# Reordering one block's VectorE queue: a sum ahead of the gain multiply, scalings behind the sums, a gain multiply one group later

## The chip, the cores and the metric

The kernel runs on one core of a Trainium2 chip. The metric is the device time of one execution in microseconds (us). Before the change it is 321.7 us, the median of 4 runs (321.48 to 322.55).

## What is computed

A linear attention without softmax is followed by a gated feed-forward layer. The batch is 8, with 8 heads, 576 tokens and a head width of 64; the layer takes the 4608 tokens as rows of 512.

```python
kv = einsum('bhsd,bhse->bhde', k, v)
o = einsum('bhsd,bhde->bhse', q, kv)
x = o / sqrt(mean(o * o, axis=-1) + 1e-06) * g_norm      # rows of 512 = 8 heads x 64
g, val = x @ w_gate, x @ w_val                            # 512 -> 1536
ffn = gelu(g) * val @ w_out                               # 1536 -> 512
out = x + sigmoid(x @ w_res) * ffn
```

## The kernel before, in words

**Blocks and batches.** The work is cut into nine blocks of 512 tokens: block b (0 to 7) is the first 512 tokens of batch b, and block 8 holds the 64 remaining tokens of every batch. While the feed-forward work of block m fills TensorE (PE), the attention of a later batch is threaded into it. Batch 2 is prepared in block 1, and batches 3 to 7 are prepared two blocks ahead, so batch 3 is begun in block 1 and finished in block 2.

**Order of the work.** There is no automatic scheduler. The program runs under a manual schedule: every engine does its instructions in the order in which they are written, and waits only where an operand or a buffer isn't ready. The order is put together from dictionaries. `at(block, slot, ...)` puts a step into a slot of a block. `aside_out(block, word, ...)` and the dictionary `amid_out` put one ahead of a named point of the output stage (`others`, in `out_by_products`). `at_word(block, i, word, ...)` puts one behind a named word of the i-th group of the gate and value stage (`gv_group`).

**The gate and value stage.** In block 2 and later it is done in three groups (i = 0, 1, 2) of 4 x 128 hidden columns. Each group computes gate (g) and value (v) by a scheme of seven half-size products instead of eight. Its order is a string of words. A digit is a product on PE (L946, 4 matmuls of 128x256). `E` is a copy of A into the bank of E on ScalarE (ACT, L956). `d` is a copy of F into SBUF on ACT (L960). `F` and `c` are sums A + d on VectorE (DVE, L967). `g11` and its like are gelus on ACT (L977). `h11`, `h12`, `h21` are products into `hid` on DVE, and `h22` is one on GpSimd (POOL), all L983. In block 2, group 0 has the order None, group 1 False, group 2 True:

```python
None:  "1g 1v Eg 5g 6g Ev 5v dg 6v dv Fg 2g Fv 2v 7g g11 7v cg 3g cv 3v h11 g12 4g g21 h12 4v g22 h21 h22"
False: "1g 1v Eg 5g Ev 5v dg 6g dv 6v Fg 2g Fv 2v 7g g11 7v cg 3g cv 3v h11 g12 4g g21 h12 4v g22 h21 h22"
True:  "1g 1v Eg 5g Ev 5v dg 6g dv 6v Fg 2g Fv 2v 7g g11 7v cg 3g cv 3v h11 g22 4g g12 h12 4v g21 h22 h21"
```

Products 1, 6, 7 and 4 all accumulate into the bank of A. So product 6 waits until the copy `E` has read A, product 7 until the sum `F` has read it, product 4 until the sum `c` has. Product 5 and then the sum `F` write the bank of F; product 2 adds to E and product 3 to F.

**Banks.** PSUM has eight banks, and all are in turn. The attention result of batch 3 (tiles `op`, o[0] to o[3]) lies in four of them at the end of block 1. In group 0 of block 2 the F tiles of g and v take the banks of o[0] and o[1]; in group 1 the A tiles of g and v take those of o[2] and o[3] (`banks_of`). From one group to the next E and F change places: the E tile of v in group 2 takes the bank of the F tile of v in group 1, and so the copy `Ev` of group 2 (L956) waits until `h12` of group 1 (L983 on DVE) has read that.

**The output stage of block 1** (`others`) does five more products of 12 matmuls (L515): wA, wE, wA, wF, wA. Its first lines, with the points at which other steps come in, are:

```python
prod(w["A"], s_[1], wo_t[:, 1], False)
aside("F")
sub(nc.vector, w["F"], w["A"], w["d"], ALU.add)
...
aside("00")
prod(w["E"], a_of(blk, 1, 2), b_of(2, 1), False)
```

The next product into wA waits until the sum into wF (L478 on DVE) has read wA. At "00" and at "end" two `token_sums` each of block 2 stand (tile `ts`, L478). The gated outputs `osb<-th,w...` (L698) stand between.

**The attention steps that matter here.** `a_norm` computes the inverse norms `ny` from the sums of squares `ss` by twelve small operations on POOL (L306 to L319). `a_t(b, i)` scales o[i] by `ny` into the tile `t` (L345, DVE) and so frees the bank of o[i]. `d_xT` sends `t` through a transposing DMA from the queue of SP into `xT` (L387). `a_g(b, j0, j1)` multiplies `xT` by the gain vector in place (L370, a DVE tensor_scalar of 128x1024 in fp16). Meanwhile POOL does `row_times_g` (L361, four operations on `t`) and in group 1 `fin` (L702, four additions on `osb`), both of 128x512.

Of the kernel before, what the change touches and what calls it, by code (L numbers as in the profile page):

```python
# [18 lines left out]
def kernel(  # L19
# [19 lines left out]
    F = moe_w_gate.shape[1]  # L39
    NP = H // 2  # L40
    NF = F // P
    NJ = 4
# [85 lines left out]
    def by_token(b, copy=nc.vector.tensor_copy, js=slice(0, NJ)):  # L128
        copy(
            out=b16_t[b, "q"].rearrange("p j h d -> p h j d")[:, :, js, :],  # L130
            in_=raw[b, "q"].rearrange("p h (j d) -> p h j d", j=NJ)[:, :, js, :],
        )
# [36 lines left out]
    def attn_begin(b):  # L169
        st[b] = {  # L170
            "qT": attnp.tile([P, NJ, NP, P], FP16, tag="qT", bufs=1, name="qT"),
            "kv2": (
                attnp.tile([P, NP, D], FP16, tag="kv2", bufs=4, name="kv2")
                if b > 0
                else t_t[B][:, NJ - 1, :].rearrange("p (r c) -> p r c", r=NP)
            ),
            "ss": attnp.tile([P, NJ + 1, H], FP32, tag="ss", name="ss"),
            "o": {},
        }
# [36 lines left out]
    def a_kv(b, copy=nc.vector.tensor_copy):  # L216
        ps = pattn.tile([P, NP, D], FP32, tag="at", name="kvp")
        kv_mm(b, ps)
        copy(out=st[b]["kv2"], in_=ps)
# [18 lines left out]
    def of_o(ap, i):  # L238

        jj, e = i // 2, i % 2  # L240
        return ap[:, 2 * jj : 2 * jj + 2].rearrange("p j (r e) -> p j r e", e=2)[:, :, :, e]
# [85 lines left out]
    def pair(b):  # L327

        return b - B // 2 if b >= B // 2 else None

    def where(b, j):
        return (b, j) if j < NJ else (B, pair(b))

    def a_t(b, i):

        o, rinv = st[b]["o"][i], st[b]["rinv"]
        if i < NJ:
            jj, e = i // 2, i % 2
            t = t_t[b][:, 2 * jj : 2 * jj + 2, :].rearrange("p j (r e d) -> p j r e d", e=2, d=D)[:, :, :, e, :]
            scale = of_o(rinv, i)[:, :, :, None].to_broadcast([P, 2, NP, D])  # L340
        else:
            t = t_t[B][:, pair(b), :].rearrange("p (h d) -> p h d", h=H)
            o = o.rearrange("p (h d) -> p h d", h=H)
            scale = rinv[:, NJ, :, None].to_broadcast([P, H, D])
        nc.vector.tensor_tensor(out=t, in0=o, in1=scale, op=ALU.mult)  # L345
# [17 lines left out]
    def a_g(b, j0, j1, eng=nc.vector):  # L363

        blk, k0 = where(b, j0)
        xs = xT_t[blk][:, k0 : k0 + j1 - j0, :, :]
        if eng is nc.scalar:
            nc.scalar.activation(out=xs, in_=xs, func=AF.Copy, scale=gcol)
        else:
            eng.tensor_scalar(out=xs, in0=xs, scalar1=gcol, scalar2=None, op0=ALU.mult)  # L370


    def d_qT(b):
        nc.sync.dma_start(
            out=st[b]["qT"].rearrange("p j c t -> p (j c) t"),
            in_=b16_t[b, "q"].rearrange("p j h d -> p (j h d)"),
            transpose=True,
        )
# [5 lines left out]
    def d_xT(b, j0, j1):  # L384
        blk, k0 = where(b, j0)
        k1 = k0 + j1 - j0
        nc.sync.dma_start(  # L387
            out=xT_t[blk][:, k0:k1, :, :].rearrange("p j c t -> p (j c) t"),
            in_=t_t[blk][:, k0:k1, :].rearrange("p j c -> p (j c)"),
            transpose=True,  # L390
        )
# [638 lines left out]
    for which in "kv":  # L1030
        if which == "k":
            t = hidp.tile([P, NF, NJ * P], FP16, tag="hid", name=which + "f").rearrange("p a b -> p (a b)")
        else:
            t = hid_s
# [8 lines left out]
    for which in "kv":  # L1043
        t = hid_of[which]
# [295 lines left out]
    amid_out = {}  # L1340
# [3 lines left out]
    def load_behind(b, x_of=None):  # L1344

        nc.gpsimd.tensor_copy(out=hold, in_=st[b]["qT"][0:1, 0, 0, 0:1])
        if x_of is not None:
            nc.gpsimd.tensor_copy(out=hold, in_=xT_t[x_of][0:1, 0, 0, 0:1])
        if pair(b) is not None:
            nc.gpsimd.tensor_copy(out=hold, in_=st[b]["qrT"][0:1, 0, 0:1])  # L1350
        load_batch(b + 1)

    def at(blk, slot, *fs):
        plans[blk].setdefault(slot, []).extend(fs)

    def aside_out(blk, ahead_of, *fs):
        amid_out.setdefault(blk, {}).setdefault(ahead_of, []).extend(fs)

    def plan_attn_2():
        b, m = 2, 1  # L1360
        act = nc.scalar.copy
        at(m - 1, 2 * NF + 3, lambda: by_token(b, act, slice(0, 2)))
        at(m, 0, lambda: by_token(b, act, slice(2, 4)), lambda: attn_begin(b), lambda: d_qT(b))
        at(m, 2, lambda: a_kv(b))
        at(m, 3, lambda: load_behind(b))
        at(m, 1, lambda: wo_sums(1))
        at(m, 3, lambda: wo_sums(3))
        at(m, 4, lambda: a_o(b))
        for j in range(NJ):
            at(m, 4 + j // 2, lambda j=j: a_ss(b, j))  # L1370
        at(m, 6, lambda: a_norm(b, 0, NJ, nc.gpsimd))
        for j in range(NJ):
            at(m, 9 + j // 2, lambda j=j: a_t(b, j))
        at(m, 10, lambda: d_xT(b, 0, NJ))
        for i in range(2):
            aside_out(m, "F", lambda i=i: a_g(b, 2 * i, 2 * i + 2))

    WHOLE = 2
    GROUPS = {blk: (1, 2) for blk in range(2, WHOLE)} | {blk: (0, 1, 2) for blk in range(WHOLE, B - 1)} | {B - 1: (1, 0, 2), B: (0, 1, 2)}
# [2 lines left out]
    def at_word(blk, i, word, *fs):  # L1382
        amid_gv.setdefault((blk, i), {}).setdefault(word, []).extend(fs)
# [5 lines left out]
    def plan_attn_ahead(b):  # L1389

        rem = pair(b) is not None
        m = b - 2
        assert rem == (m in GROUPS)
        act, pool = nc.scalar.copy, nc.gpsimd
        begin = [lambda: attn_begin(b), lambda: d_qT(b)]
        if rem:
            at_word(m, 0, "h22", begin.pop(0), lambda: d_rem_qT(b))
        if m in GROUPS:
            for i in range(2):
                half = lambda i=i: by_token(b, act, slice(2 * i, 2 * i + 2))  # L1400
                if whole(m):
                    at_word(m, i, "g11", half)
                else:
                    at(m, 2 + i, half)
            if whole(m):
                at_word(m, 1, "g11", *begin)
            else:
                at(m, 3, *begin)
            if b + 1 < B:
                at(m, 2 * GF, lambda: load_behind(b))  # L1410
            last = len(GROUPS[m]) - 1
        else:
            at(m, 8, lambda: by_token(b, act, slice(0, 2)))
            at(m, 9, lambda: by_token(b, act, slice(2, 4)), *begin)
            at(m, NF - 1, lambda: a_kv(b, act))
            at(m, NF, lambda: load_behind(b))
        if rem:
            at_word(m + 2, 0, "cv", lambda: a_g(b, NJ, NJ + 1))
            own = 2 * pair(b) + 1 == b
            at_word(m, last, "5v" if own else "3g", lambda: a_rem_kv(b))  # L1420
            at_word(m, last, "dv" if own else "g12", lambda: kv_out(b))
            if own:
                at_word(m, last, "3g", lambda: rem_mm(b))
            at_word(m, last, "g12", lambda: rem_out(b))
        else:
            at(m, NF, lambda: a_o(b), lambda: a_ss(b, 0), lambda: a_ss(b, 1))
            aside_out(m, "D", lambda: a_ss(b, 2), lambda: a_ss(b, 3))
        aside_out(m, "F", lambda: a_norm(b, 0, NJ + rem, pool))
        first = [lambda: new_block(b), lambda: a_t(b, 0), lambda: a_t(b, 1)]
        if whole(m + 1):  # L1430
            aside_out(m, "01" if m + 1 == WHOLE else "11", *first[0:2])
            amid_out[m].setdefault("end", []).insert(0, first[2])
        else:
            at(m, NF + 3, *first)
        if whole(m + 1):
            t = [lambda j=j: a_t(b, j) for j in range(NJ)]
            if rem:
                at_word(m + 1, 0, "h21", lambda: a_t(b, NJ), lambda: d_xT(b, NJ, NJ + 1))
            for i, word, fs in (
                (0, "1v", t[2:3]),  # L1440
                (0, "Fv", [t[3], lambda: d_xT(b, 0, NJ)]),
                (1, "cv", [lambda: a_g(b, 0, 2)]),
                (2, "Fv", [lambda: a_g(b, 2, NJ)]),
            ):
                at_word(m + 1, i, word, *fs)
            return
        for j in range(2, NJ + rem):
            at(m + 1, j - 2, lambda j=j: a_t(b, j))
        at(m + 1, 1, lambda: d_xT(b, 0, NJ))
        at_word(m + 1, 1, "Fv", lambda: a_g(b, 0, 2))  # L1450
        at_word(m + 1, 1, "cv", lambda: a_g(b, 2, NJ))
# [12 lines left out]
    for blk in GROUPS:  # L1464
        t = token_sums(blk, nc.vector)
# [170 lines left out]
```

## Time and profile before

| what | value |
|---|---|
| median of 4 runs | 321.7 us (321.48 to 322.55) |
| time of the profiled execution | 330.97 us |
| its span, first to last instruction | 329.2 us |
| PE, DVE, ACT, POOL busy in the span | 314.6 (96%), 279.8 (85%), 210.9 (64%), 186.4 (57%) us |
| mean granted PE clock | 0.989 |
| 4 matmuls of 128x256 back to back (chain) | 0.44 us |
| 12 of them (chain) | 1.31 us |
| block 1's last products and block 2, and where block 3 begins | 82.31 to 124.89 us |

The profile is of one execution. Its span runs from the first instruction to the last; 1.77 us of its time lie outside. A row of the timeline gives the start, the time from start to end, the engine, the line in the code, the operation, the tile written and the tiles read; in brackets stands how long the engine had been idle and what ended that. The chain of waits is followed back from the last instruction: each piece is what the next one had to wait for, or what preceded it on the same engine. Where a piece of four matmuls takes longer than 0.44 us, PE waited in it.

### The profile page before, as it was taken

The page shows a single profiled execution, that of the slowest core. Times are in us where ns is not written, and L with a number is a line of the kernel's source. Part 1 is how long each engine was busy: PE and PEld are TensorE (multiplying, and loading weights), DVE is VectorE, ACT ScalarE, POOL GpSimd, SP SyncE. Part 2 cuts the span into 40 slices and gives each one's busy share as a digit, 9 for nine tenths or more (in the row PEclk, how much of TensorE's full clock was granted, in tenths as well). Part 3 has the DMA queues.
Part 4 walks back from the last instruction along what each step waited for, and adds up shares of the span by engine and source line. Part 5 has one row for each costly group of instructions (what it writes and reads, how often), then busy time and mean ns, then how long its engine had stood idle before and what let it go on. Part 6 is the DMA issues. An engine that isn't in the chain of part 4 may idle for free.

```text
span 329.2 us, 7756 instructions
## 1 busy us (share of the span) xinstructions
PE 314.6 (96%) x3044; PEld 248.2 (75%) x3044; DVE 279.8 (85%) x486; ACT 210.9 (64%) x385; POOL 186.4 (57%) x249
## 2 busy tenths in 40 slices
PE   8899999999999999999999999999999999399993
PEld 3545755445888888888888888888888888268882
DVE  6788889798897999899989997999896778947774
ACT  3773676465568776877687678766764668026770
POOL 3792342573778568866786678147812753805432
PEclk9999999999999999999999999999999999959999
DMA  7999999899977594669366937202400030000304
GB/s 247 323 190 204 194 205 174 179 201 135 197 77 94 163 191 53 124 162 188 53 132 155 182 37 164 96 2 55 155 2 0 3 128 2 0 2 7 122 0 129
DMA packets 76694, 38.90 MB, mean 118 GB/s; under 512 B 42098, under 2 KB 74354, under 8 KB 76658
## 3 DMA queue, kind: packets, MB, share of 16 engines
q0 software_dynamic: 38752, 17.17, 41.4%
q1 hardware_dynamic: 37328, 20.71, 24.8%
q8 instruction: 24, 0.39, 0.5%
q10 hardware_dynamic: 578, 0.52, 0.5%
q14 instruction: 12, 0.10, 0.1%
HBM read 38.80 MB, written 9.44 MB: 147 GB/s over the span
## 4 chain that ended last, share of the span: by engine, by line
PE 90%; DVE 5%; DMA 2%; SPq 1%; issue 1%; POOL 0%; ACT 0%; DVEq 0%
PE Av L946 12%; PE Ag L946 12%; PE wA L515 11%; PE Fv L946 6%; PE Fg L946 6%; PE gps L410 5%; PE vps L410 5%; PE rA L566 4%; PE fps L447 3%; PE Ev L946 3%; PE Eg L946 3%; PE wE L515 3%; PE wD L515 3%; PE w L515 2%; PE wF L515 2%; DVE ts L478 2%
## 5 line engine op out<-in xcount | busy, mean ns | idle before, releaser
L983 POOL TENSOR_TENSOR hid<-ge,c 128x512 f16<-128x512 f16 x22 | 25.6, 1162 | 49.6 <-ACT ge L977 49.6
L515 PEld LDWEIGHTS <-hid_s 128*128 128x128 f16 x384 | 37.5, 98 | 4.5 <-issue 0.2
L946 PEld LDWEIGHTS <-wsv 128*128 128x128 f16 x352 | 34.2, 98 | 5.8 <-issue 1.3
L946 PEld LDWEIGHTS <-wsg 128*128 128x128 f16 x352 | 34.7, 99 | 4.4
L515 PEld LDWEIGHTS <-hid 128*128 128x128 f16 x288 | 28.7, 100 | 10.2 <-issue 6.2
L361 POOL TENSOR_TENSOR t<-t,g 128x512 f16<-128x512 f16 x32 | 35.9, 1151 | 0.0
L956 ACT COPY Eg<-Ag 128x512 f32<-128x512 f32 x22 | 12.8, 583 | 35.7 <-PE Ag L946 35.7
L702 POOL TENSOR_TENSOR osb<-osb,t 128x512 f32<-128x512 f32 x28 | 34.1, 1248 | 0.0
L946 PEld LDWEIGHTS <-wg 128*128 128x128 f16 x264 | 26.0, 99 | 3.4
L967 DVE TENSOR_TENSOR Fg<-Ag,d 128x512 f32<-128x512 f32 x22 | 15.3, 697 | 15.5 <-ACT d L960 7.6
L946 PEld LDWEIGHTS <-wv 128*128 128x128 f16 x264 | 26.0, 99 | 3.2
L946 PE MATMUL Av<-ts,wsv 128*128 128x256 f16 x176 | 26.4, 272 | 0.2 <-ACT Ev L956 0.2
L946 PE MATMUL Ag<-ts,wsg 128*128 128x256 f16 x176 | 26.4, 273 | 0.0
L258 DVE TENSOR_REDUCE ss<-sq 128x8 f32<-128x512 f32 x32 | 20.5, 679 | 1.7 <-ACT sq L253 1.7
L398 ACT ACTIVATE ge<-gps 128x512 f16<-128x512 f32 x20 | 11.7, 597 | 14.3 <-PE gps L410 14.1
L515 PE MATMUL wA<-wo_ts,hid_s 128*128 128x256 f16 x168 | 20.6, 273 | 0.0
L977 ACT ACTIVATE ge<-Eg 128x512 f16<-128x512 f32 x22 | 13.1, 597 | 10.2 <-PE Eg L946 10.2
L345 DVE TENSOR_TENSOR t<-op,ny 128x512 f16<-128x512 f32 x28 | 18.4, 684 | 0.5 <-POOL ny L319 0.4
L977 ACT ACTIVATE ge<-c 128x512 f16<-128x512 f32 x22 | 13.8, 626 | 7.8 <-DVE c L967 7.8
L967 DVE TENSOR_TENSOR c<-Ag,d 128x512 f32<-128x512 f32 x22 | 15.2, 689 | 4.2 <-PE Ag L946 4.2
L977 ACT ACTIVATE ge<-Fg 128x512 f16<-128x512 f32 x22 | 13.0, 591 | 8.6 <-PE Fg L946 6.6
L410 PE MATMUL gps<-xT,wg 128*128 128x512 f16 x72 | 18.5, 379 | 0.0
(219 smaller groups left out, 865.8 us busy)
## 6 DMA issues: line engine op xcount, KB each, us to landing
out_dram<-osb SPq DMA_DIRECT2D x14, 512.0 KB, 3.6
qraw<-in_q_dram POOLq DMA_DIRECT2D x7, 512.0 KB, 6.6
k<-in_k_dram POOLq DMA_DIRECT2D x7, 512.0 KB, 8.7
v<-in_v_dram POOLq DMA_DIRECT2D x7, 512.0 KB, 10.6
wg<-in_moe_w_gate_dram POOLq DMA_DIRECT2D x2, 512.0 KB, 8.2
wv<-in_moe_w_val_dram POOLq DMA_DIRECT2D x2, 512.0 KB, 9.1
wo<-in_moe_w_out_dram POOLq DMA_DIRECT2D x2, 512.0 KB, 14.1
out_dram<-osb SPq DMA_DIRECT2D x4, 256.0 KB, 4.5
```

The source lines that it names most:

```text
L258: nc.vector.tensor_reduce(out=out_, in_=sqs.pop((b, i)), op=ALU.add, axis=mybir.AxisListType.X)
L345: nc.vector.tensor_tensor(out=t, in0=o, in1=scale, op=ALU.mult)
L361: eng.tensor_tensor(out=t_t[blk][:, jj, :], in0=t_t[blk][:, jj, :], in1=g16, op=ALU.mult)
L410: nc.tensor.matmul(ps[:, j0 * P : j1 * P], lhsT=w[:, cc, :], rhs=xT_t[blk][:, j0:j1, cc, :], start=(cc == 0 and j0 == 0), stop=(cc == NP - ...
L515: nc.tensor.matmul(ps[:, e - es[0], :], lhsT=a[:, f, e * P : (e + 1) * P], rhs=b[:, f, :], start=(start and e == es[0] and f == 0), stop=( ...
L566: nc.tensor.matmul(out_[:, e, :], lhsT=x_[:, e, cc, :], rhs=w_[:, cc, :], start=(first and e == 0 and cc == 0), stop=(cc == 1), skip_group ...
L702: nc.gpsimd.tensor_tensor(out=res_all[of], in0=res_all[of], in1=t_t[blk][of], op=ALU.add)
L946: nc.tensor.matmul(out_[:, r, :], lhsT=lhsT, rhs=rhs, start=(first and r == 0 and c == 0), stop=(c == 1), skip_group_check=True,)
L956: nc.scalar.copy(out=tile_of("E", u), in_=ps["A", u])
L967: nc.vector.tensor_tensor(out=dst, in0=ps["A", u], in1=sb["d", u], op=ALU.add)
L977: nc.scalar.activation(out=ge[q], in_=source(q, "g"), func=AF.Gelu)
L983: eng.tensor_tensor(out=dst, in0=ge[q], in1=source(q, "v"), op=ALU.mult)
```

## The change

Four steps change place; none is added or taken away.

- Batch 2's two gain multiplies (`a_g`, L370) stood ahead of the sum into wF in block 1's output stage. They now stand behind it, ahead of the first two token sums ("00").
- Batch 3's scaling of o[2] stood behind `1v` in group 0 of block 2, ahead of `Fg`. It now stands behind `Fv`.
- Batch 3's scaling of o[3], with the transposing DMA that follows it, stood behind `Fv`. It now stands behind `cv`.
- Batch 3's first gain multiply stood behind `cv` in group 1 of block 2, ahead of `h11`. It now stands behind `h21`.

On DVE, the order of block 1's end and of block 2's groups 0 and 1 changes accordingly. On PE the first matmul of `1v` of group 1 now has a wait for DVE of its own, for the bank of o[3]. On POOL, ACT and SP the order is the same.

```diff
@@ plan_attn_2
         for i in range(2):
-            aside_out(m, "F", lambda i=i: a_g(b, 2 * i, 2 * i + 2))
+            amid_out.setdefault(m, {}).setdefault("00", []).insert(i, lambda i=i: a_g(b, 2 * i, 2 * i + 2))
@@ plan_attn_ahead
             if rem:
                 at_word(m + 1, 0, "h21", lambda: a_t(b, NJ), lambda: d_xT(b, NJ, NJ + 1))
+            first_whole = m + 1 == WHOLE
             for i, word, fs in (
-                (0, "1v", t[2:3]),
-                (0, "Fv", [t[3], lambda: d_xT(b, 0, NJ)]),
-                (1, "cv", [lambda: a_g(b, 0, 2)]),
+                (0, "Fv" if first_whole else "1v", t[2:3]),
+                (0, "cv" if first_whole else "Fv", [t[3], lambda: d_xT(b, 0, NJ)]),
+                (1, "h21" if first_whole else "cv", [lambda: a_g(b, 0, 2)]),
                 (2, "Fv", [lambda: a_g(b, 2, NJ)]),
             ):
                 at_word(m + 1, i, word, *fs)
```

## The prediction

> **What bounds the kernel now.** I read the page's shares first, then its chain of waits by engine.
>
> ```profile
> span 329.2 us, 7756 instructions
> ...
> PE 90%; DVE 5%; DMA 2%; SPq 1%; issue 1%; POOL 0%; ACT 0%; DVEq 0%
> ```
>
> PE carries 90% of the chain. So the change can give back only time in which PE waits for DVE in the stretch it touches, and can lose only by making new waits of that kind. Next I read the chain of waits piece by piece from 84 to 112 us. There 4 matmuls take 0.44 us and 12 take 1.31 where nothing is awaited; these pieces are longer:
>
> ```profile
> 87.55 1.47 PE wA L515 x12
> ...
> 93.39 0.48 PE Fv L946 x4
> ...
> 95.18 0.56 PE Ag L946 x4
> 95.75 0.00 issue
> 95.75 0.60 PE Av L946 x4
> ...
> 105.55 0.51 PE Fv L946 x4
> 106.07 0.01 issue
> 106.07 0.58 ACT Ev L956
> 106.65 0.04 issue
> 106.69 0.60 PE Av L946 x4
> ```
>
> The excesses are: (a) 0.16 at the third wA; (s) 0.04 at 5v of group 0; (b) 0.12 + 0.16, say 0.29, at 7g and 7v of group 0; (d) from 105.55 to 107.29 (the end of the last piece) 1.74 for two pieces that need 0.875, so 0.865, at 5v and 6v of group 2. Two small ones lie between and behind: (c) 0.03 at a piece of 0.47 (97.66, 4v of group 0) and (e) 0.09 at a piece of 0.53 (108.60, 7v of group 2). Together about 1.48 us. Who is late is told by the timeline of DVE in the same stretch, with the POOL and ACT rows that count:
>
> ```profile
> 86.02 0.88 DVE L370 TENSOR_SCALAR xT<-xT,gcol 128x1024 f16<-128x1024 f16 x2
> 86.81 0.69 DVE L478 TENSOR_TENSOR wF<-wA,wd 128x512 f32<-128x512 f32 x1
> ...
> 92.54 0.68 DVE L345 TENSOR_TENSOR t<-op,ny 128x512 f16<-128x512 f32 x1
> ...
> 93.81 0.68 DVE L345 TENSOR_TENSOR t<-op,ny 128x512 f16<-128x512 f32 x1
> 94.41 0.69 DVE L967 TENSOR_TENSOR Fg<-Ag,d 128x512 f32<-128x512 f32 x1
> ...
> 100.01 4.50 POOL L702 TENSOR_TENSOR osb<-osb,t 128x512 f32<-128x512 f32 x4
> ...
> 103.30 1.49 DVE L370 TENSOR_SCALAR xT<-xT,gcol 128x1024 f16<-128x1024 f16 x1
> ...
> 105.31 0.68 DVE L983 TENSOR_TENSOR hid<-ge,Fv 128x512 f16<-128x512 f16 x1
> ...
> 108.39 0.48 DVE L370 TENSOR_SCALAR xT<-xT,gcol 128x1024 f16<-128x1024 f16 x1
> ```
>
> The two gain multiplies hold the wF sum until 86.81, though its product ended near 86.3. The scaling at 93.81 holds Fg until 94.41, though its operand from ACT is there at 93.78. The gain multiply at 103.30 takes 1.49 us, where its twin at 108.39, with POOL at rest, takes 0.48: it ends only after POOL's four additions (104.51). It makes h12 late (ends 105.99), Ev starts behind that at 106.07, and PE waits for Ev: that is (d).
>
> **Which time the sum is made against.** The profiled execution took 330.97 us (span 329.2, 1.77 outside), 9.3 more than the median 321.7. Most of that is one DVE row in block 7, which no part of the change names:
>
> ```profile
> 279.51 7.67 DVE L478 TENSOR_TENSOR ts<-xT 128x512 f16<-128x512 f16 x1
> ```
>
> Behind it PE begins its next gate stage at 291.49 where the four preceding products alone would lead to 284.03: 7.46 us. Its first four pieces then take 0.85 instead of 0.44 (1.65 more). Together 9.1 of the 9.3. I therefore take the stretch before 279 as valid for the runs behind the median, and subtract the change from 321.7.
>
> **The change, part by part.**
>
> *Sum into wF first.* DVE is free at 86.10 (end of the sums of squares), the product ends near 86.3; the sum of 0.69 then ends near 87.0, well ahead of 87.4, when PE could start the third wA. So (a), 0.16, goes there. But it is not kept: 5v of group 0 waits for the scaling of o[1] (92.54 to 93.22; 5v starts at 93.28), and that is the end of an unbroken DVE row t, osb, osb, t that starts at 90.74, when POOL has `ny` (its last operation ends at 90.70, and DVE idles 0.39 us for it). PE arrives 0.16 earlier and waits 0.16 longer. Gain of this part: 0, unless POOL's norm moves.
>
> Does it? The moved multiplies (0.88) and the token sums behind them (0.42 and 0.43 at 87.41 and 87.86) now run as one row from 87.0 to about 88.7, beside the same POOL operations. Between 86.19 and 88.36 before, POOL's took 0.38, 0.31, 0.24, 0.57 and 0.34, later ones 0.22 to 0.29: 0.6 to 0.7 us lost to four such DVE operations. Moved by 0.7 us, the same four cost about the same, so `ny` stays within 0.2 of 90.70 and this part within -0.2 and +0.2. On DVE the next step, osb<-wA, waits for PE until 88.9; a late row has 0.2 to spare there, and the wait at 90.35 has 0.39 more. The Trainium skill, "SBUF — State Buffer", section "Who interferes with whom", speaks against this: a DVE operation in a two-port mode, or with two SBUF inputs against a POOL operation that reads SBUF, and the POOL operation block one another, and the later one waits for the whole instruction. By that rule each of the four could wait for one POOL operation of 0.25, 1.0 in all: the row ends at 89.7, 0.6 past its spare, less than 0.39 later than `ny` needs, perhaps 0.2 on PE. By the rows the token sums in the midst of POOL's chain took 0.42 and 0.43, no more than elsewhere, and POOL waited. I take the rows: 0.
>
> *Scalings of o[2] and o[3] later.* Fg starts when the second token sum ends, about 93.85, not 94.41, and ends at 94.55; Fv waits for ACT's copy (93.96 + 0.59) and runs from 94.6 to 95.3. 7g could start at 95.05 and 7v at 95.47, both behind these: (b), 0.29, goes. Then DVE steps on by 0.6 per operation: o[2] 95.2, cg 95.8, cv 96.4 to 97.1, o[3] 97.0 to 97.7, h11 97.6, h12 98.2, h21 98.8 to 99.5. 4v, which waits for cv (c), now could start at 97.2, so (c) goes too. h11 to h21 are 0.2 later than before, while PE is 0.32 earlier. Their takers: 5v of group 1 at 98.95 needs h11 (98.3), Ev of group 1 needs h12 (98.9) and was at 99.22, used by 6v only at about 100. DVE's next work is Fg near 100.1, so 0.6 of slack covers all this. The new wait: the first product of `1v` in group 1 needs o[3] read at 97.7; it would start at 98.08. Behind it on PE stands everything, so it costs from the point where o[3] is over 0.35 late. The transposing DMA is issued at 97.75 instead of 96.3; with 4.3 us to landing (6.9 at most) it lands at 102.1 to 104.6. Behind it in SP's queue stand the transposes of qr (98.44 before, now about 99.8, first read by PE at 109.5) and of q (102.89, which waits for ACT's copy anyway). Cost 0.
>
> *Gain multiply behind h21.* Without it h11 starts at 103.0, h12 at 103.65 when its gelu is done, h21 at 104.25 to 104.9. h12 is done at 104.3, before `Ev` of group 2 could start (104.7), h11 at 103.7, before 5v (105.1). (d) goes, 0.865. But POOL doesn't rest at 104.9: its h22 (1.17 us, started at 105.04) would start near 104.75. By the row at 103.30 the multiply ends about 0.3 after POOL's operation, at 106.2; by the row of 0.48 at 105.4. The skill's rule agrees with 106.2. I take 106.2. Then Fg of group 2, whose product ends near 106.25, is not held, and PE needs it only at 107.3. The cover is thus some 0.3 us: 7g and 7v of group 2 start at 107.3 and 107.75, with Fg and Fv done at 107.0 and 107.6. Beyond it, each further 0.1 us is lost. (e), the late Fv of group 2, goes as well: in block 3, where Fg of its group 2 comes with DVE idle for 0.60 before it, no piece of the chain is over 0.44. Cost 0, bounds 0 to 0.5 (if the multiply waited a second time).
>
> *Sum.* (b) 0.29 + (c) 0.03 + (d) 0.865 + (e) 0.09 = 1.27 us. After 112 us the chain is PE to the end of block 7 and the loads are issued behind PE's own progress, so it is carried through. Rounding down for the thin covers, 1.2: 321.7 - 1.2 = 320.5 us.
>
> **The rivals.**
>
> *Half only: the stall moves.* The multiply behind h21 waits for POOL's h22 and more, or for a late landing, and holds Fg of group 2 into 107.9 or so: 0.6 of (d) comes back. 321.7 - 0.65 = 321.05. For it: cover of only 0.3. Against it: h22 is a single operation, and block 3's multiply beside POOL (136.35, 0.87 us) cost PE nothing.
>
> *Nothing: the gap is filled elsewhere.* PE reaches block 3 1.2 earlier, but a later wait isn't PE's, so 321.7. Against it: blocks 3 to 6 have only PE in their chain, with one common excess of 0.17 at 5v of group 0, where `ny` of the next batch binds, and that hangs on PE's products too.
>
> *Slower: DVE is starved beside the norm chain.* The row of 7.67 shows a DVE operation that waited while POOL went through eight `t` operations without a break. If the moved multiplies got no turn until POOL's norm ends (about 90.1), they would end at 91.0, the token sums at 91.75, then osb, osb, t, osb, osb, t at 0.6 each lead to 95.4, so 5v starts at 95.45, not 93.28: +2.17, less the 1.27: +0.9, 322.6. It decides from the point where the multiplies end after 89.5, and turns the whole slower from a delay of 1.3 at 5v. Against it: POOL's small operations stand 0.07 to 0.12 us apart, and the token sums among them were not held.
>
> **How the numbers follow.** Main case (320.1 to 320.9): 0.62, likeliest 320.5. Half: 0.17. Nothing: 0.09. Slower: 0.12, of which most is the starving or an unseen wait of that size, up to 323. A measurement of this kernel can tell about 0.3%, 1.0 us, from no change. Faster by more than that (under 320.7) holds most of the main case and some of the better end: 0.58; within: 0.31; slower (over 322.7): 0.11. Range: 320.0 (all of 1.48, with 0.2 more) to 322.0, which leaves out the slower case and a little below.
>
> **What would show it.** In the chain after: the third wA at 1.31; 5v of group 0 at 0.6 or so, still behind the scaling of o[1]; 7g and 7v of group 0 at 0.44; no ACT piece near 106; Ev of group 2 behind its own 1v. In the timeline: the multiply of group 1 at 1.3 or so beside POOL's h22, and Fg of group 2 right behind it. Wrong it would be if `ny` came after 91.0, if a piece of block 2 behind 105 us were still over 0.5, or if the first 1v of group 1 waited.

## The result and the profile after

The changed kernel takes 320.97 us, the median of 44 runs, beside 321.95 us for the kernel before in 63 runs of the same sitting. The ratio is 0.9962 with a 95% interval of 0.9951 to 0.9974, that is 0.84 to 1.58 us less. A later sitting gave 0.9975 (0.9961 to 0.9989), 0.35 to 1.25 us less. The forecast of 1.2 us less lies in both.

Some executions are slowed throughout, as the first profiled one of the changed kernel was (405.96 us, at a granted PE clock of 0.757), so the lines here are of another execution of the same kernel, 320.45 us, at 0.996. Its page begins and sums up its chain of waits thus:

```profile
span 318.7 us, 7756 instructions
...
PE 96%; DVE 3%; issue 0%; DVEq 0%
```

This is the chain of waits in the stretch that was shown of before (start, time, what). Read it against 0.44 us for four matmuls and 1.31 us for twelve:

```profile
87.14 1.31 PE wA L515 x12
...
92.81 0.48 PE Fv L946 x4
...
94.60 0.44 PE Ag L946 x4
95.04 0.44 PE Av L946 x4
...
104.64 0.44 PE Fv L946 x4
105.08 0.44 PE Ag L946 x4
105.52 0.44 PE Av L946 x4
```

Every excess but one is gone: the third wA, 7g and 7v of group 0, and in group 2 the products 5v, 6g, 6v follow one another with no ACT piece between. Only 5v of group 0 keeps its 0.04. The timeline of the same execution has the DVE rows that answer to those of before, with three of POOL and ACT:

```profile
85.93 0.70 DVE L478 TENSOR_TENSOR wF<-wA,wd 128x512 f32<-128x512 f32 x1 [0.25 <-PE wA L515]
86.54 0.87 DVE L370 TENSOR_SCALAR xT<-xT,gcol 128x1024 f16<-128x1024 f16 x2
...
89.87 0.26 POOL L319 TENSOR_TENSOR ny<-nh,ny 128x32 f32<-128x32 f32 x1
...
91.96 0.68 DVE L345 TENSOR_TENSOR t<-op,ny 128x512 f16<-128x512 f32 x1
...
93.24 0.70 DVE L967 TENSOR_TENSOR Fg<-Ag,d 128x512 f32<-128x512 f32 x1
...
104.13 1.16 POOL L983 TENSOR_TENSOR hid<-ge,c 128x512 f16<-128x512 f16 x1 [0.49 <-ACT ge L977]
104.19 1.38 DVE L370 TENSOR_SCALAR xT<-xT,gcol 128x1024 f16<-128x1024 f16 x1
104.46 0.56 ACT L956 COPY Ev<-Av 128x512 f32<-128x512 f32 x1
105.62 0.70 DVE L967 TENSOR_TENSOR Fg<-Ag,d 128x512 f32<-128x512 f32 x1
```

The sum into wF now waits for PE alone. Fg of group 0 starts when the token sums end. The gain multiply of group 1 does meet POOL's h22, which starts 0.06 us ahead of it, and takes 1.38 us; Fg of group 2 starts right behind it, and PE doesn't wait.

**How the runs are compared.** The times of one kernel lie up to 2.3 us apart in one sitting (320.31 to 322.61 for the changed kernel), which is more than is at stake. One profile shows a source of this that the change doesn't touch, the kernel's opening: in the run of the multiply alone (below), PE waited 6.86 us for the transposing DMA of q (74.23 to 81.09) ahead of every changed instruction. So each run is also measured by a stretch of its own profile: from the first product wD of block 1 to that of block 2, in the chain of waits. Before it is 83.62 to 117.03, 33.41 us; after it is 83.21 to 115.60, 32.39 us, that is 1.02 less. A stretch is of one execution, but it repeats well: the next one, from block 2 to block 3, which most of the experiments leave as it was, takes 32.52 or 32.53 us in eight profiles at full clock. The lowest time of each run agrees with it: 321.28 before and 320.31 after in one sitting, 0.97 less.

### The profile page after: what moved, and what is told of

Read it like the earlier page. It is cut to its first block, busy times and chain, and to the rows that moved or that the text cites. A ratio compares the mean times of both kernels' runs of the same rounds, so it can differ in the third digit from the quotient of the medians.

```text
span 404.1 us, 7756 instructions
## 1 busy us (share of the span) xinstructions
PE 397.0 (98%) x3044; PEld 281.4 (70%) x3044; DVE 282.9 (70%) x486; ACT 217.4 (54%) x385; POOL 185.9 (46%) x249
## 4 chain that ended last, share of the span: by engine, by line
PE 97%; DVE 2%; ACT 0%; issue 0%; DVEq 0%
PE Av L946 12%; PE Ag L946 12%; PE wA L515 12%; PE Fv L946 6%; PE Fg L946 6%; PE gps L410 5%; PE vps L410 5%; PE rA L566 4%; PE fps L447 3%; PE Ev L946 3%; PE Eg L946 3%; PE wD L515 3%; PE wF L515 3%; PE wE L515 3%; PE w L515 3%; PE rps L430 2%
## 5 line engine op out<-in xcount | busy, mean ns | idle before, releaser
L515 PEld LDWEIGHTS <-hid_s 128*128 128x128 f16 x384 | 42.5, 111 | 12.0
L946 PEld LDWEIGHTS <-wsg 128*128 128x128 f16 x352 | 39.0, 111 | 10.6
L946 PEld LDWEIGHTS <-wsv 128*128 128x128 f16 x352 | 38.8, 111 | 10.6
L515 PEld LDWEIGHTS <-hid 128*128 128x128 f16 x288 | 32.5, 113 | 8.6 <-issue 0.3
L946 PE MATMUL Ag<-ts,wsg 128*128 128x256 f16 x176 | 32.8, 318 | 0.0
L946 PE MATMUL Av<-ts,wsv 128*128 128x256 f16 x176 | 32.8, 319 | 0.0
L515 PE MATMUL wA<-wo_ts,hid_s 128*128 128x256 f16 x168 | 26.3, 320 | 0.0
L410 PE MATMUL vps<-xT,wv 128*128 128x512 f16 x72 | 23.8, 464 | 0.0
L399 DVE TENSOR_TENSOR hid<-ge,vps 128x512 f16<-128x512 f16 x20 | 13.7, 687 | 14.3 <-PE vps L410 12.1
L410 PE MATMUL gps<-xT,wg 128*128 128x512 f16 x72 | 23.4, 459 | 0.0
```

The source lines that it names most:

```text
L399: nc.vector.tensor_tensor(out=hids[blk][:, f, :], in0=ge, in1=vps, op=ALU.mult)
L410: nc.tensor.matmul(ps[:, j0 * P : j1 * P], lhsT=w[:, cc, :], rhs=xT_t[blk][:, j0:j1, cc, :], start=(cc == 0 and j0 == 0), stop=(cc == NP - ...
L515: nc.tensor.matmul(ps[:, e - es[0], :], lhsT=a[:, f, e * P : (e + 1) * P], rhs=b[:, f, :], start=(start and e == es[0] and f == 0), stop=( ...
L946: nc.tensor.matmul(out_[:, r, :], lhsT=lhsT, rhs=rhs, start=(first and r == 0 and c == 0), stop=(c == 1), skip_group_check=True,)
```

## The experiments

| kernel | ratio to before (95%) | lowest, and of before beside it | stretch wD to wD |
|---|---|---|---|
| before | 1 | 321.24 to 321.33 | 33.41 |
| whole change | 0.9975 (0.9961 to 0.9989) | 320.31, 321.28 | 32.39 |
| sum first alone | 0.9998 (0.9986 to 1.0009) | 321.15, 321.28 | 33.24 |
| scalings alone | 0.9977 (0.9964 to 0.9990) | 320.46, 321.28 | - |
| scalings alone, again | 0.9990 (0.9968 to 1.0013) | 320.49, 321.24 | 32.54 |
| multiply alone | 1.0001 (0.9988 to 1.0015) | 320.84, 321.28 | 32.88 |
| change without the multiply's move | 0.9968 (0.9955 to 0.9982) | 320.20, 321.24 | 32.38 |
| before, POOL at rest | 0.9993 (0.9977 to 1.0009) | 320.74, 321.24 | 32.86 |
| before, POOL nudged once | 1.0000 (0.9980 to 1.0019) | 320.81, 321.33 | - |
| before, POOL nudged three times | 1.0000 (0.9979 to 1.0022) | 320.85, 321.27 | 32.88 |
| later scalings everywhere | 1.0150 (1.0121 to 1.0179) | 325.45, 321.24 | 32.40 |
| order everywhere, clear of POOL | 0.9976 (0.9959 to 0.9993) | 320.46, 321.33 | 32.40 |
| order in blocks 2 to 4 | 0.9967 (0.9945 to 0.9990) | 319.94, 321.27 | 32.40 |

Each lowest time has that of before in the same sitting beside it. A dash stands where no stretch was taken from the profile.

**The whole change, and its three parts one by one.** The first is the changed kernel. The next three make one part of the diff above each: its first hunk (the sum), the two scalings of its second hunk, and that hunk's multiply.

> The whole change once more, for a profile with a full PE clock. My theory (PE waits for DVE at three places, and the later places keep what they gain): 1.2 us less than before; in the chain the third wA of block 1 at 1.31, 5v of group 0 of block 2 held by the scaling of o[1] until about 93.28, then no piece over 0.50 up to the remainder's products; the gain multiply of group 1 beside POOL's h22, about 1.3 us long. Rival (the stall moves): the multiply holds Fg of group 2 and a piece of 0.5 to 1 us over its need stands at 7g of group 2; some 0.6 us less than before.

The main theory holds but for one piece: 5v of group 0 is not held until 93.28, it starts at 92.69 in the timeline. No piece of four matmuls is over 0.50 up to the remainder's products, and the multiply lasts 1.38. The rival's piece at 7g of group 2 isn't there.

> Only the sum into wF goes ahead of batch 2's gain multiplies; the rest is as before. My theory: the 0.16 us at the third wA goes and comes back at 5v of group 0, which waits for the scaling of o[1], which waits for POOL's norm: time the same within 0.2 us. Rival (starved DVE): the multiplies wait in POOL's norm chain, the norm ends after 91.0 and 5v starts after 93.5: slower by 0.3 to 1 us.

The stretch is 0.17 shorter. So the gain of 0.16 was neither given back, as I had it, nor turned into a loss, as the rival had it. The time alone could not tell (the interval takes in no change); the stretch and the lowest time (0.13 less) do.

> Only the scalings of o[2] and o[3] go behind Fv and cv; the rest is as before. My theory: 7g and 7v of group 0 lose their 0.29 us of waiting, but the multiply of group 1 still ends with POOL's four additions, whose time is set by token sums and not by PE, so that most of it is given back as a longer wait for Ev of group 2: 0.1 to 0.2 us less than before. Rival (the parts add up): 0.32 us less, with the wait before Ev of group 2 unchanged at about 0.6 us.

The time fell by 0.3 to 1.2 us and the lowest by 0.82, where 0.1 to 0.2 was expected and 0.32 by the rival. The profiled execution took 651.32 us, so the cause is read from another profile of this kernel, below.

> Only batch 3's first gain multiply goes behind h21 of group 1; the rest is as before. My theory: the wait of 0.86 us at 5v and 6v of group 2 goes, and the 0.09 behind it: 0.95 us less than before, with 7g and 7v of group 0 still 0.29 us late. Rival (the stall moves to Fg of group 2, behind a multiply that waits for POOL's h22): 0.3 us less.

The stretch is 0.53 shorter: neither the 0.95 of my theory nor the 0.3 of the rival. The wait before Ev is gone, and the multiply takes 1.39 beside POOL's h22, but there were only 0.43 + 0.09 us to win. Why is told in the section on the prediction. The median shows nothing of it, which the opening told of above accounts for in the profiled execution; that it does so in all the others is not shown.

**Why the scalings alone gave so much.**

> The same kernel as in the run of the scalings alone, for a profile with a full PE clock and for a second measurement; that run gave 0.75 us less than before, where I had expected 0.1 to 0.2. From the first product wD of block 1 to that of block 2 before took 33.41 us. New theory (which side of a POOL boundary the multiply meets): with PE 0.3 us earlier against POOL's four additions, the multiply of group 1 comes ahead of the third or fourth of them, gets in between, and takes 0.9 us instead of 1.49; then 6v of group 2 hardly waits, and the stretch is 0.75 to 0.85 shorter. Rival (my old one): it still ends behind the fourth, and the stretch is 0.2 to 0.35 shorter.

> The changed kernel with batch 3's first gain multiply back behind cv of group 1: sum into wF first, and scalings behind the sums. If the multiply's place gives nothing once the scalings are moved: the stretch from wD to wD 0.95 to 1.02 us shorter than 33.41, the time as for the whole change. If the multiply's place holds a gain of its own: 0.4 to 0.5 us longer than the whole change, with a wait for Ev of group 2 in the chain.

Both times the size is met: 32.54 is 0.87 shorter, and 32.38 is as short as the whole change. The ratio of the second measurement of the scalings alone (0.9990) takes in no change and can't tell; its lowest time is 0.75 less. The multiply's own place gives nothing once the scalings are moved. But the multiply does not take the 0.9 us that I expected. In the second of these kernels the multiply behind cv and POOL's four additions stand thus in the timeline:

```profile
98.96 4.75 POOL L702 TENSOR_TENSOR osb<-osb,t 128x512 f32<-128x512 f32 x4
102.22 0.48 DVE L370 TENSOR_SCALAR xT<-xT,gcol 128x1024 f16<-128x1024 f16 x1
```

It takes 0.48, as with POOL at rest, and the four additions take 4.75 instead of 4.50: now POOL waits. A narrow window of the same timeline shows the fourth addition alone, and it is the one that waits (1.40 instead of 1.16):

```profile
102.30 1.40 POOL L702 TENSOR_TENSOR osb<-osb,t 128x512 f32<-128x512 f32 x1
```

In the kernel before, a like window gives:

```profile
103.35 1.16 POOL L702 TENSOR_TENSOR osb<-osb,t 128x512 f32<-128x512 f32 x1
```

There the multiply started at 103.30, 0.05 us ahead of the fourth addition, and missed; here it starts 0.08 us ahead and gets in. In the second profile of the scalings alone it is 0.08 again (102.49 and 102.57), with 0.48. And the sum first alone, whose multiply stands where it stood in the kernel before, missed again with 0.05:

```profile
102.60 1.49 DVE L370 TENSOR_SCALAR xT<-xT,gcol 128x1024 f16<-128x1024 f16 x1
...
102.65 1.16 POOL L702 TENSOR_TENSOR osb<-osb,t 128x512 f32<-128x512 f32 x1
```

That is the whole wait (d): whether the multiply gets in ahead of POOL's last addition or waits for its end.

**Is it POOL at all?** The next two change nothing in DVE's order of before.

```diff
-            nc.gpsimd.tensor_tensor(out=res_all[of], in0=res_all[of], in1=t_t[blk][of], op=ALU.add)
+            if blk != 1:
+                nc.gpsimd.tensor_tensor(out=res_all[of], in0=res_all[of], in1=t_t[blk][of], op=ALU.add)
```

> The kernel before, with POOL's four additions of block 1 (L702) left out, so that block 1's stored output lacks the term x; its DVE order is that of before. If the multiply of group 1 is long because POOL is at work: it takes 0.48 us, no wait for Ev stands in group 2, and the stretch from wD to wD is 0.5 us shorter than 33.41 (0.43 at 5v and 6v and 0.09 at 7v), the time too. If it is long for another reason, or h12 is late from DVE's own load: nothing changes.

The multiply takes 0.48 (at 103.44), Ev of group 2 (105.51) follows ACT's copy Eg without a gap, and the stretch is 0.55 shorter (the lowest time 0.50; the ratio can't tell). DVE's own load is thus no cause of (d). The next adds work to POOL instead:

```diff
+            if blk == 1 and jj == (1, 1):
+                nc.gpsimd.tensor_copy(out=hold, in_=x_sums[blk + 1][0:1, 3, 1, 1, 0:1])
             nc.gpsimd.tensor_tensor(out=res_all[of], in0=res_all[of], in1=t_t[blk][of], op=ALU.add)
```

> The kernel before, with one more operation: a copy of one element on POOL, 0.2 us, ahead of its four additions in block 1; DVE, PE and ACT have the order of before. If the multiply of group 1 is long because it comes 0.05 us ahead of the boundary between POOL's third and fourth addition and misses it: with the boundary 0.2 later it gets in between them, takes 0.5 to 0.65 us, the fourth addition waits, and the stretch from wD to wD is 0.4 to 0.55 shorter than 33.41, the time too, though work was added. If a multiply beside POOL's additions always waits for their end: 1.6 us, and the stretch is 0.1 to 0.2 longer.

This is a miss. All but one of 22 times are no lower than 321.45, so one copy seldom freed the multiply, if ever; the one at 320.81 is as low as where the multiply gets in. In the profiled execution (PE clock 0.948) the multiply started 0.07 us ahead of the fourth addition's start as worked out (105.15 against 101.88 plus three times 1.115) and took 1.51. What happened at full clock is not seen. With three copies in a row:

> The kernel before with three such copies of one element on POOL (some 0.45 us in all) ahead of its four additions in block 1. In the run with one copy the profile fell on a lower PE clock and the multiply again started 0.07 us ahead of a boundary and missed it, and the time was not shorter. In blocks 3 and 4 of the kernel before the multiply starts 0.54 us ahead of a boundary, gets in there and takes 0.87. With three copies it should start 0.4 to 0.5 ahead of one here too. If the moment of its start decides: it takes 0.75 to 0.9, no wait for Ev or one under 0.1 is left, the stretch from wD to wD is 0.4 to 0.55 shorter than 33.41. If a multiply beside this row of additions waits for its end: 1.9 us, the stretch 0.3 to 0.45 longer.

```profile
100.39 4.68 POOL L705 TENSOR_TENSOR osb<-osb,t 128x512 f32<-128x512 f32 x4
103.08 0.97 DVE L370 TENSOR_SCALAR xT<-xT,gcol 128x1024 f16<-128x1024 f16 x1
```

The multiply gets in after a short wait (0.97, a little over what I expected), no ACT piece stands in the chain, and the stretch is 32.88, 0.53 shorter, with three operations more than before. So the wait doesn't come from the amount of POOL's work: with more of it, at another moment, the wait is gone. The lowest time agrees (0.42 less). The ratio is 1.0000; but POOL at rest, where there is nothing to wait for, has 0.9993, so the ratios don't show in how many executions the multiply gets in.

**Carrying the order to later blocks.** In the changed kernel 5v of group 0 still waits 0.17 us in each of blocks 3 to 6 for the scaling of o[1]. The edit gives these blocks block 2's order of scalings and token sums, and makes POOL's gain products wait for the last token sum:

```diff
-            if blk + 1 == WHOLE or blk + 1 == LAST[0]:
+            if whole(blk + 1) or blk + 1 == LAST[0]:
                 nc.gpsimd.tensor_copy(out=hold, in_=x_sums[blk + 1][0:1, 3, 1, 1, 0:1])
...
+            late = True
             for i, word, fs in (
-                (0, "Fv" if first_whole else "1v", t[2:3]),
-                (0, "cv" if first_whole else "Fv", [t[3], lambda: d_xT(b, 0, NJ)]),
+                (0, "Fv" if late else "1v", t[2:3]),
+                (0, "cv" if late else "Fv", [t[3], lambda: d_xT(b, 0, NJ)]),
...
-        for key, f in zip(("00", "00", "22", "01") if whole(blk) else ("00", "22", "01", "11"), t):
+        for key, f in zip(("00", "00", "end", "end") if whole(blk) else ("00", "22", "01", "11"), t):
```

> The changed kernel, with the same order given to blocks 3 to 6: the scalings of o[2] and o[3] behind Fv and cv, the last two token sums behind the scaling of o[1] instead of amid POOL's norm, and POOL's gain products behind the last token sum. In these blocks 5v of group 0 waits 0.17 us for the scaling of o[1]. If POOL's norm, slowed by token sums, sets that: the 0.17 goes in each of four blocks, 0.5 to 0.7 us less than the changed kernel, 1.5 to 1.7 less than before. If the later work on DVE (the long scaling of the remainder behind h21) then holds Fg of group 1: 0.2 to 0.4 us lost in each block, slower than the changed kernel by 0.2 to 0.9.

Slower by 1.2 to 1.8%, and mostly for a reason that neither expectation named. Block 3 has the gain: from wD to wD of the next block 32.35 instead of 32.52. Blocks 4 and 6 lose 2.03 and 2.05 us, block 5 0.94. POOL's four gain products now start later, and in block 4 the remainder's gain multiply meets them:

```profile
158.20 4.49 POOL L361 TENSOR_TENSOR t<-t,g 128x512 f16<-128x512 f16 x4
...
161.10 1.74 DVE L370 TENSOR_SCALAR xT<-xT,gcol 128x512 f16<-128x512 f16 x1
```

It takes 1.74 us instead of 0.34, until POOL's row is over (162.69), and every sum behind it on DVE is late. In block 6 it is the same (229.38, 1.74). In block 5 the multiply starts at the same place in POOL's row, 0.44 us ahead of the fourth product, and gets in:

```profile
195.68 0.62 DVE L370 TENSOR_SCALAR xT<-xT,gcol 128x512 f16<-128x512 f16 x1
```

What is lost there is nearer to the second expectation, though more than its 0.2 to 0.4: `Fg` of group 1 starts at 200.09, when the long scaling of the remainder (198.61, 1.55) is over, and 7g and 7v behind it take 0.60 each.

The next edit keeps this order and moves the gain multiplies to group 2 (the lines that differ from the last edit):

```diff
-            at_word(m + 2, 0, "cv", lambda: a_g(b, NJ, NJ + 1))
+            at_word(m + 2, 2, "cv", lambda: a_g(b, NJ, NJ + 1))
-                (1, "h21" if first_whole else "cv", [lambda: a_g(b, 0, 2)]),
+                (2, "Fv", [lambda: a_g(b, 0, 2)]),
```

> The order of the last attempt in blocks 3 to 6 (scalings behind the sums, two token sums behind the scaling of o[1], POOL's products behind them), but with all gain multiplies of blocks 2 to 7 in group 2: both of the batch behind Fv, the remainder's behind cv, where POOL has nothing to do in the profile of before. If the 4.8 us of the last attempt came from the remainder's multiply meeting POOL's four products: that goes, and the 0.17 at 5v of four blocks is gained: 320.2 to 319.4. If the long scaling of the remainder, or three multiplies in one group, hold DVE's next sum: 321 to 323.

The collision is gone (blocks 3 and 4: 32.35 each, from wD to wD), but block 5 takes 33.09 instead of 32.76 and block 6 30.38 instead of 30.30, so that the lowest time is 0.87 less than before beside it, where the changed kernel's was 0.97 less. In block 5's group 2 the chain runs through DVE and ACT for 8 us, from Fg at 203.40 over the two multiplies (204.61, 0.87) and the sum c. So the second expectation holds there, and the first in blocks 3 and 4. The last kernel keeps both lessons: this order in blocks 2 to 4 only.

> The order of the last attempt (scalings behind the sums, two token sums behind the scaling of o[1], gain multiplies in group 2) in blocks 2 to 4 alone, with blocks 5 and 6 as before: in block 5, which also holds the long chain for the last remainder, three multiplies in group 2 held DVE's sums and cost 0.3. If block 3 and 4 keep their 0.17 each and block 5 loses nothing: 1.3 to 1.4 us less than before, 0.3 to 0.4 less than the changed kernel. If what was gained ahead of block 5 is lost to a new meeting with POOL there: as the changed kernel.

The stretches of blocks 2 to 5 are 32.40 (wD of block 1 to that of block 2), 32.35, 32.35 and 32.77. Its lowest time is 319.94, 1.33 less than before beside it; the changed kernel, measured in another sitting, was 0.97 less than before beside it. Its ratio to before is 0.9967 (0.9945 to 0.9990), faster than before; that it beats the changed kernel rests on the stretches and the lowest times, since the intervals of the two overlap and the two were not run side by side.

## Why the prediction was right, and which steps were not

**The time and the sign were right.** 320.5 was forecast as 1.2 less than before, and 0.84 to 1.58 less was measured. All of it lies in the stretch that was named, and blocks 3 to 6 take what they took before (32.52, 32.54, 32.76 and 30.30 in the profile after). Leaving out the row of 7.67 us in block 7 was right too: the same token sum takes 1.00 in the profile after (278.06), though nothing was changed there.

**The sum was near in part by luck.** The pieces give (a) 0.16, (b) 0.29, (c) 0.03, (d) 0.43 and (e) 0.09, together 1.00; the stretch fell by 1.02. I had 0 for (a) and 0.865 for (d), 1.27 in all: one error took back a third of the other, and rounding down to 1.2 some more.

*(d) was mis-sized.* The step that failed is "1.74 for two pieces that need 0.875". Between 5v and 6v of group 2 the order has a third product, 6g. It ran while PE's chain was following ACT, and so the chain doesn't list it. The timeline of before has it:

```profile
105.44 0.61 PE L946 MATMUL Fv<-ts,wsv 128*128 128x256 f16 x4
105.89 0.60 PE L946 MATMUL Ag<-ts,wsg 128*128 128x256 f16 x4
...
106.07 0.57 ACT L956 COPY Ev<-Av 128x512 f32<-128x512 f32 x1 [0.62 <-PE Fv L946]
106.69 0.60 PE L946 MATMUL Av<-ts,wsv 128*128 128x256 f16 x4 [0.20 <-ACT Ev L956]
```

Three products in 1.74 us need 1.31, so 0.43 was lost. The multiply alone (0.53 with (e)) and POOL at rest (0.55) both measured this. (The bracket of `Ev` names 5v, which ended at about the same moment as h12. But in the profile after `Ev` starts at 104.46 and 5v at 104.48, so `Ev` doesn't need 5v, and in the once nudged kernel the bracket of the same `Ev` names DVE's `hid`. What it waited for here is h12, as forecast.)

*(a) was kept.* The step that failed is "PE arrives 0.16 earlier and waits 0.16 longer", and under it "the same four cost about the same". POOL's norm took 4.51 us before (86.19 to 90.70) and 4.35 after (85.78 to 90.13), 0.16 less, so the scaling of o[1] came earlier by just what PE had gained, and 5v waits 0.04 as before. The bound of plus or minus 0.2 held this; the value that I took in it was wrong. It is the sum's place that does this: the norm takes 4.33 to 4.35 in six profiles with the sum first, and 4.49 to 4.51 in six without. In the first six, POOL's first two operations take 0.21 to 0.22 each, beside the sum; in the others 0.37 to 0.38 and 0.31 to 0.32, beside the gain multiplies. Why the same operations cost POOL less at the later place was not tested.

*(b) and (c) were right,* in place and size, and so was the slack for h11, h12 and o[3]: no new wait appeared at 1v of group 1.

*The multiply behind h21 was right in its duration* (1.38, forecast 1.3): it ended 0.28 us after POOL's h22, as the row of 1.49 had it. Fg starts right behind it, and PE doesn't wait. But the move was not needed. The prediction read the row of 1.49 as "it ends only after POOL's four additions", which is true of that execution, and took it as fixed. With the scalings moved the multiply starts 0.03 us earlier against POOL's row, and in both profiles of that it gets in. So the 0.52 of (d) and (e) came in those kernels without the step that it was credited to, and the parts do not add up: 0.17, 0.87 and 0.53 by the stretches, and 1.02 for all.

**The rivals.** None came. Against the half case, 7g and 7v of group 2 take 0.44 each behind the moved multiply; against the starved DVE, the two moved multiplies took 0.87 amid POOL's norm, 0.88 before; against a gap filled elsewhere, blocks 3 to 6 kept their times.

## What to carry to other kernels

A wait in the chain is worth what the order needs between its two ends, so lay the order of the waiting engine beside the chain before sizing it: work done during the wait is not listed. A duration beside a POOL row is not a fixed cost: before moving a DVE operation away from such a row, see how far its start is from the boundary between two POOL operations, because an edit elsewhere may move it over that boundary. When the edits of a change are judged one by one, use a stretch of the profile that holds only them; here ratios from 14 runs hid 0.5 to 0.9 us.

## What the runs showed of the hardware

A DVE gain multiply and POOL's row of additions hold each other up. Started 0.05 us ahead of the next addition the multiply missed and took 1.49 (two profiles); 0.08 us ahead it got in and took 0.48 while POOL waited 0.25 (two profiles). Started 0.54 to 0.65 us ahead it got in behind the running addition (0.87 in blocks 3 to 6 of before, 0.97 in the thrice nudged kernel).

The start as the profile gives it does not decide alone. Beside POOL's gain products three multiplies of 128x512 started 0.44 us ahead of the fourth product and took 1.74, 0.62 and 1.74 (blocks 4, 5 and 6 of the later scalings everywhere). The token sum of block 7 started 0.70 us ahead of the next product in the kernel before and took 7.67, until POOL's whole row was over; in the order in blocks 2 to 4 it started 0.70 ahead too and took 1.02.

The Trainium skill, "SBUF — State Buffer", section "Who interferes with whom", says that the second to issue blocks until the first has finished; that fits the 0.97 and the 1.38 beside a single operation, but a waiting operation that lets several POOL operations pass ahead of it goes beyond what it states. What decides between one operation and the whole row is left open.
